# Retention and wave-MLP in one kernel: all batches by chunk pairs, loads in 512-byte rows, transposes moved from TensorE to DMA

## Chip, cores, metric

One core of one Trainium2 chip. The metric is the device time of one launch in microseconds; lower is better.

## The reference, cut to what matters

```python
# retention, for B=4, H=8, S=768, D=64: one state (D x D) per batch and head
state = gamma * state + k_t^T v_t
y_t = (1/sqrt(D)) * q_t @ state
# y becomes x (4, 768, 512); then the wave-MLP block
theta = x @ w_theta
zr, zi = x * cos(theta), x * sin(theta)
u = x + w_tok_r @ zr + w_tok_i @ zi        # over the 768 tokens of a batch
out = u + relu(u @ w_ch)
```

The recurrence is computed in chunks of 128 tokens: A = masked K Q^T inside a chunk, Y = A V, I = the part from the state, S = the update of the state. The MLP block works on 24 tiles of 128 tokens; a tile needs z of all six chunks of its batch.

## The kernel before

Batch 0 is already done by *pairs* of chunks: 256 tokens are loaded as 128 partitions with two neighbouring tokens each, so a DMA row is 512 bytes, and the products use quarters (64 by 64) of the array. Batches 1 to 3 load one chunk at a time in 256-byte rows. One queue (SP) issues nearly all DMA.

```python
def load_chunk(n):                                   # batches 1 to 3
    for name, src in (("kf", k), ("qf", q), ("vf", v)):
        t = io.tile([P, H, D], FT, name=name, bufs=7)
        nc.sync.dma_start(out=t, in_=src[b, :, c * P:(c + 1) * P, :].rearrange("h s d -> s h d"))
def load_pair(g): ...                                # batch 0: "h (p two) d -> p h (two d)"

def att_T(n):                                        # k and q by TensorE: 8 transposes + a copy
    for i, src in enumerate((s["kb"], s["qb"])):
        for j in range(NP):
            nc.tensor.transpose(kq_ps[:, i * NP + j, :], src[:, j * P:(j + 1) * P], ident)
    nc.vector.tensor_copy(kqT, kq_ps)
def att_T_dma(n):                                    # ... by DMA: only n >= 19 (batch 3)
    nc.sync.dma_start_transpose(out=kqT, in_=s["kqb"]...)
# ... x: TensorE for n < 19, DMA after. u: TensorE for tiles m < 12, DMA after.

for s_ in range(last_slot):                          # one chunk and about one tile per slot
    load_chunk(n + 5)                                # loads run five chunks ahead
    moe_U_dma / att_T(n) / att_Z(n - 3) / moe_M(first half) / att_prep(n + 1)
    att_Yinter(n - 1) / att_A(n) / att_Y(n - 1) / moe_M(second half) / moe_O / att_X(n - 2)
```

## Time and profile before

| | before |
|---|---|
| time, median (lowest to highest) | 181.78 us (181.23 to 185.89, 4 runs) |
| profiled span, mean granted clock | 180.0 us, 0.99 |
| PE busy, DVE busy, ACT busy | 91%, 60%, 43% |
| 128x128 transposes on TensorE (k and q, x, u) | 152, 76, 52 |

Engines are named as in the profile: PE is TensorE, DVE VectorE, ACT ScalarE, POOL GpSimd, SP the engine that issues DMA. A step from one PE instruction's start to the next is what it costs; the "busy" length of one is longer (0.38 us for products that start 0.22 us apart). The lines that the argument starts from stand in the prediction.

### The profile page before, as it was taken

To read this page: it belongs to the slowest core of one execution; us is meant where nothing else is said; L and a number is where in the kernel's file an instruction comes from. 1 tells how busy PE (TensorE), PEld (TensorE's weight loads), DVE (VectorE), ACT (ScalarE), POOL (GpSimd) and SP (SyncE) were. 2 spreads that over 40 slices of the span, in tenths; PEclk is the share of its full clock that TensorE was granted. 3 is DMA by queue.
4 is the path that set the end of the run, shared out by engine and by line. 5 is a ranking of instruction groups with operands and counts; after the bars stand their busy time and mean duration, and the time that the engine had idled before them with its cause. 6 is when DMAs were issued, how large, how long until landed. Compare 5 with 4: busy or idle time off the path is not lost.

```text
span 180.0 us, 3837 instructions
## 1 busy us (share of the span) xinstructions
PE 163.8 (91%) x1511; PEld 93.6 (52%) x1538; DVE 107.8 (60%) x153; ACT 77.3 (43%) x143; POOL 74.6 (41%) x102
## 2 busy tenths in 40 slices
PE   7889886796989699999999999999999999999990
PEld 2355563544556365665565556455544544444560
DVE  2266776654754777878676676575645644434441
ACT  6426664451059745746362464346445332200010
POOL 6284557298786687657663562250000000000000
PEclk9999999999999999999999999999999999999997
DMA  4999999999989999999999799945464363334643
GB/s 136 310 329 329 298 364 230 285 303 212 285 181 273 206 218 227 274 256 229 220 244 247 147 228 192 196 87 120 117 117 109 95 103 92 99 94 112 110 127 118
DMA packets 85906, 35.64 MB, mean 198 GB/s; under 512 B 70912, under 2 KB 80384, under 8 KB 85888
## 3 DMA queue, kind: packets, MB, share of 16 engines
q1 hardware_dynamic: 85744, 35.27, 83.7%
q8 instruction: 12, 0.20, 0.5%
q10 hardware_dynamic: 144, 0.13, 0.2%
q14 instruction: 6, 0.05, 0.1%
HBM read 25.69 MB, written 6.29 MB: 178 GB/s over the span
## 4 chain that ended last, share of the span: by engine, by line
PE 82%; DVE 6%; ACT 5%; issue 3%; DVEq 0%; ACTq 0%
PE y_ps L425 31%; PE o_ps L453 11%; PE th_ps L396 11%; PE yT_ps L360 3%; PE at_ps L331 3%; PE y_ps L545 3%; PE kq_ps L202 3%; PE st_ps L368 3%; PE x_ps L393 2%; PE yT_ps L349 2%; PE kq_ps L236 2%; PE u_ps L436 2%; PE y_ps L495 1%; ACT stbd L319 1%; DVE at L255 1%
## 5 line engine op out<-in xcount | busy, mean ns | idle before, releaser
L425 PE MATMUL y_ps<-z,wti 128*128 128x512 bf16 x136 | 51.5, 379 | 0.7 <-issue 0.2
L425 PE MATMUL y_ps<-z,wtr 128*128 128x512 bf16 x127 | 48.1, 379 | 2.5 <-DVE z L407 2.1
L401 ACT ACTIVATE cs<-th_ps,halfpi 128x512 bf16<-128x512 f32 x24 | 16.5, 687 | 35.1 <-PE th_ps L396 32.8
L407 DVE TENSOR_TENSOR z<-cs,x_sb 128x1024 bf16<-128x1024 bf16 x24 | 19.1, 798 | 15.8 <-ACT cs L402 15.8
L335 DVE TENSOR_TENSOR at<-at_ps,mask 128x1024 bf16<-128x1024 f32 x18 | 22.0, 1220 | 6.0 <-PE at_ps L331 6.0
L396 PE MATMUL th_ps<-wth,xT 128*128 128x512 bf16 x90 | 24.0, 379 | 0.3
L453 PE MATMUL o_ps<-wch,uT 128*128 128x512 bf16 x88 | 23.1, 379 | 0.2
L430 DVE TENSOR_TENSOR u<-y_ps,x_sb 128x512 bf16<-128x512 f32 x23 | 15.8, 690 | 12.5 <-PE y_ps L425 12.5
L193 POOL TENSOR_TENSOR vb<-vf,vsc 128x512 bf16<-128x512 f32 x18 | 19.5, 1085 | 6.2 <-PE yT_ps L360 3.5
L456 DVE SCALAR_TENSOR_TENSOR ot<-o_ps,u 128x512 f32<-128x512 f32 x23 | 15.9, 691 | 10.1 <-PE o_ps L453 9.9
L425 PEld LDWEIGHTS <-wti 128*128 128x128 bf16 x138 | 13.5, 98 | 16.2 <-issue 3.6
L191 POOL TENSOR_TENSOR kqb<-qf,qsc 128x512 bf16<-128x512 f32 x18 | 19.7, 1096 | 5.1 <-DMA qf<-in_q_dram 5.0
L425 PEld LDWEIGHTS <-wtr 128*128 128x128 bf16 x138 | 13.5, 98 | 13.5
L319 ACT CAST stbd<-st_ps 64x256 bf16<-64x256 f32 x40 | 14.6, 366 | 11.9 <-PE st_ps L308 11.4
L190 POOL CAST kqb<-kf 128x512 bf16<-128x512 f32 x18 | 11.7, 650 | 15.3 <-PE st_ps L368 9.8
L402 ACT ACTIVATE cs<-th_ps,zerob 128x512 bf16<-128x512 f32 x24 | 16.3, 681 | 0.0
L376 ACT CAST xT<-yT_ps 128x512 bf16<-128x512 f32 x18 | 10.5, 585 | 8.7 <-PE yT_ps L360 7.4
L453 PEld LDWEIGHTS <-uT 128*128 128x128 bf16 x92 | 8.8, 98 | 9.9 <-ACT uT L438 0.2
L468 POOL CAST wrow<-wtok 128x768 bf16<-128x768 f32 x12 | 10.2, 862 | 8.6 <-PE w_ps L475 6.2
L205 DVE COPY kqT<-kq_ps 128x1024 bf16<-128x1024 bf16 x13 | 9.0, 689 | 6.2 <-PE kq_ps L202 6.2
L396 PEld LDWEIGHTS <-xT 128*128 128x128 bf16 x96 | 8.6, 98 | 6.8
L545 PE MATMUL y_ps<-warm 128*128 128x512 bf16 x26 | 9.7, 497 | 1.5 <-DVE warm L124 1.3
(79 smaller groups left out, 195.2 us busy)
## 6 DMA issues: line engine op xcount, KB each, us to landing
out_dram<-ot SPq DMA_DIRECT2D x23, 256.0 KB, 2.3
kf<-in_k_dram SPq DMA_DIRECT2D x18, 256.0 KB, 4.9
qf<-in_q_dram SPq DMA_DIRECT2D x18, 256.0 KB, 5.3
vf<-in_v_dram SPq DMA_DIRECT2D x18, 256.0 KB, 5.5
wtok<-in_moe_w_tok_r_dram SPq DMA_DIRECT2D x6, 384.0 KB, 5.8
wtok<-in_moe_w_tok_i_dram SPq DMA_DIRECT2D x6, 384.0 KB, 5.5
pair<-in_k_dram SPq DMA_DIRECT2D x3, 512.0 KB, 8.1
pair<-in_q_dram SPq DMA_DIRECT2D x3, 512.0 KB, 9.1
```

The lines of the kernel that those rows point to most:

```text
L191: nc.gpsimd.tensor_mul(qb.rearrange(r3, h=H), raw[n, "qf"], _bcast_last(qsc[:, c], D))
L193: nc.gpsimd.tensor_mul(vb.rearrange(r3, h=H), raw[n, "vf"], _bcast_last(vsc[:, c], D))
L319: nc.scalar.copy(stbd[(c + 1) % 2][sl, :, sl], st_ps[b][sl, :, sl])
L335: nc.vector.tensor_mul(at.rearrange("p a j t -> p (a j) t"), at_ps.rearrange("p a j t -> p (a j) t"), _bcast_mid(mask, H))
L396: nc.tensor.matmul(th_ps, s["xT"][:, j, :], wth[:, j, :], start=(j == 0), stop=(j == NP - 1))
L401: nc.scalar.activation(cs[:, 0, :], th_ps, AF.Sin, bias=halfpi, scale=1.0)
L402: nc.scalar.activation(cs[:, 1, :], th_ps, AF.Sin, bias=zerob, scale=1.0)
L407: nc.vector.tensor_mul(zs[b][:, c], st[n]["cs"], _bcast_mid(xs[b][:, c, :], 2))
L425: nc.tensor.matmul(y_ps, wT[r][:, s0, t0 * P:(t0 + 1) * P], zs[b][:, s0, r, :], start=(s0 == 0 and r == 0), stop=(s0 == nT - 1 and r == 1))
L430: nc.vector.tensor_add(u, y_ps, xs[b][:, t0, :])
L453: nc.tensor.matmul(o_ps, mo[m]["uT"][:, j, :], wch[:, j, :], start=(j == 0), stop=(j == nD - 1))
L456: nc.vector.scalar_tensor_tensor(ot, o_ps, 0.0, mo[m]["u"], ALU.max, ALU.add)
```

## The change

The intent: give all batches the pair form that batch 0 has, with one slot per pair (two chunks, two tiles), and take transposes off TensorE, which is busy to the end.

```diff
-    def load_chunk(n): ...            # 256-byte rows, bufs=7 per input
+    def load(n, name):                # any pair, 512-byte rows, 7 buffers in all
+        t = io.tile([P, H, 2 * D], FT, name="pair", bufs=7)
+        nc.sync.dma_start(out=t, in_=src[b, :, 2 * g * P:2 * (g + 1) * P, :].rearrange(
+            "h (p two) d -> p h (two d)", two=2))
+    def flip_dma(n, name):            # k or q of a pair, 128x1024
+        nc.sync.dma_start_transpose(out=t.rearrange("p w j t -> p (w j) t"), in_=...)
+    def x_dma(n):                     # x of a pair, 128x1024
+        nc.sync.dma_start_transpose(out=xs[b][:, 2 * g:2 * g + 2, :]..., in_=st[n, "xT"]...)
-    moe_U (TensorE, m < 12), att_X (TensorE, n < 19), att_T (TensorE, n < 19)
+    # u: moe_U_dma but for the last tile.  x: TensorE only for pairs 0-2.  k, q: TensorE only for pairs 0-3.
-            nc.tensor.matmul(st_ps[b][:, j, :], s["kb"][:, j * P:(j + 1) * P], ...)   # 128x128
+            nc.tensor.matmul(st_ps[b][par * D:(par + 1) * D, j, :], ...)              # 64x64 x4
@@ the slot of pair n (cut to the order in which SP meets its work) @@
+        load(n + 2, "k")
+        for t in done: moe_U_dma(t)          # tiles of the slot before
+        prep(n + 1, "q", PP); prep(n + 1, "v", PP)
+        ret_I(n - 1, 1)
+        ret_A(n, 0); ret_mask(n, 0)          # needs kT, qT of pair n
+        ret_Y(n - 1, 1); ret_S(n - 1, 1); ret_out(n - 1, 0, ...); ret_out(n - 1, 1, ...)
+        x_dma(n - 1)                         # waits for ScalarE's copies of xT
+        load(n + 2, "q")
+        prep(n + 1, "k", K); flip_dma(n + 1, "k")
+        moe_M(mine[0] ...); theta(n - 1, 0); moe_u(mine[0])
+        load(n + 2, "v")
+        flip_dma(n + 1, "q")
+        theta(n - 1, 1); ret_S(n, 0); ret_A(n, 1); ret_mask(n, 1); ret_Y(n, 0); ret_I(n, 0)
+        moe_M(mine[1], 0, nT)
+        zmul(n - 1, 0); zmul(n - 1, 1); moe_u(mine[1])
+        for t in done: moe_O(t); moe_out(t)
```

Slots run from 3 to 12, slots 5 and 6 with one tile. Loads of pairs 5 to 11 are issued in slots 3 to 9. In the prologue the cast of k of pair 2 on ScalarE also moved to an earlier place.

## The prediction

> **What bounds the kernel now.** I read, in this order, the page's table of busy slices, the busy time by windows, the waits, the timeline of TensorE and the list of DMA issues.
>
> ```profile
> PE   7889886796989699999999999999999999999990
> PEclk9999999999999999999999999999999999999997
> DMA  4999999999989999999999799945464363334643
> ```
>
> Each digit is a slice of 4.5 us. From slice 13 (about 58 us) to the end TensorE is never under 90% busy and its clock is full; before that it has holes. The DMA engines are full from 5 us to about 115 us, then half empty. So two resources are full together for the first two thirds, and a change that moves work from one to the other has to be costed on both.
>
> ```profile
> 20.00:40.00 20.00, 15.96 (x238) 10.55 (x240) 14.60 (x20) 11.15 (x19) 11.57 (x12) 1.00 1.12 294
> 60.00:80.00 20.00, 19.60 (x203) 12.16 (x207) 16.04 (x24) 10.71 (x21) 14.39 (x15) 1.00 1.10 240
> 80.00:100.00 20.00, 19.84 (x202) 12.06 (x205) 14.72 (x21) 10.73 (x21) 10.98 (x12) 1.00 1.07 234
> 140.00:160.00 20.00, 19.89 (x118) 9.51 (x119) 9.44 (x14) 5.59 (x10) 0.00 (x0) 1.00 0.41 93
> ```
>
> Columns: stretch, busy time of PE, PEld, DVE, ACT, POOL, then clock, DMA share, GB/s. The full DMA moves 294 GB/s while 512-byte rows (batch 0) are loaded, 234 to 240 with 256-byte rows. In the waits, PE waits 0.2 us in all between 62 and 176 us, and about 9 us between 8 and 62 us, on DVE and ACT results. It does not wait for a load, since loads run up to five chunks ahead. So the end is set by TensorE's work, with DMA hidden by prefetch.
>
> Busy PE is not PE at its peak, so I cost PE from distances between starts:
>
> ```profile
> 21.19 0.42 PE L251 MATMUL at_ps<-kqT 64*64 64x128 bf16 x16 [0.24 <-DVE at L255]
> 21.41 0.42 PE L271 MATMUL yT_ps<-at,kqb 64*64 64x128 bf16 x16
> 21.77 0.40 PE L285 MATMUL yT_ps<-kqT,stbd 128*128 128x128 bf16 x4
> ...
> 103.09 0.61 PE L202 MATMUL kq_ps<-ident,kqb 128*128 128x128 bf16 x8
> 103.54 0.38 PE L425 MATMUL y_ps<-z,wtr 128*128 128x512 bf16 x1
> 103.75 0.38 PE L425 MATMUL y_ps<-z,wti 128*128 128x512 bf16 x1
> ```
>
> Eight transposes hold PE 0.45 us (56 ns each); a 512-column product 215 ns; sixteen products on 64 by 64 tiles 0.22 us, or 0.36 us when the next group has another tile size.
>
> **What the Trainium skill says.** "TensorE: Matmul & The Clock Gate", Part 1: a warm matmul starts every N / 2.4 GHz + 2.5 ns, 215.7 ns for 512 and 55.6 for 128 columns; the trace agrees. "TensorEngine Tiling (Array Packing)", Key Properties: tiles run independently, but a change of tiling mode drains the array; the trace agrees (14 ns per 64 by 64 product, and 0.13 us more at a change). "DMA: Bandwidth & Descriptors", Specifications: line rate wants at least 512 bytes. The trace agrees in direction only: 256-byte rows still reach about 80% of the rate of 512-byte rows. Same page, Queues, rings and completion order: each DMA engine takes descriptors in ring order, so with everything issued from one queue a load issued first delays a transpose issued after it. The kernel before shows it as late landings (below).
>
> **The change on TensorE.** Removed are transposes. Of k and q: 104 + 48 on the page, after it 4 pairs x 16 = 64, so 88 fewer. Of x: 76, then 24 (pairs 0 to 2), 52 fewer. Of u: 52, then 4, 48 fewer. 188 x 56 ns = 10.5 us, all on the path. The attention work is about equal: for two chunks before, A 2 x 0.33, Y 2 x 0.35, S 2 x 0.23, I 0.45 = 2.3 us; for a pair after, 6 groups of 16 at 0.22, three changes of mode and I 0.45 = 2.2 to 2.5. Products y, theta and o do not change. A steady slot (one pair, two tiles) is then 24 x 0.216 + 8 x 0.216 + 8 x 0.216 + 2.3 = 10.9 us, and I add 0.3 for theta waiting behind the ACT copies of xT: 11.2, where the kernel before takes 11.8 to 12.6 for two chunks. DVE sheds 11 kq copies of 0.69 and 13 x copies of 0.41 (about 13 us), ACT trades 12 uT copies (7.0 us) for k casts of 1.04 per pair; neither was the bound. With nothing else, 181.7 - 10.5 = about 171 us.
>
> **The change on DMA.** Costs over 16 engines from the packet records of the trace before. Saturated between 60 and 70 us, 8230 packets of 256 bytes: 16 x 10 us / 8230 = 19.4 ns apiece, so a chunk load (1024 packets) is 1.24 us. Between 4 and 24 us, taking out 512 packets of 2 KB at 85 ns and 320 of 3 KB at 121 ns, 8318 packets of 512 bytes cost 28.6 ns, so a pair load (1024 packets) is 1.83 us. Half the packets, three quarters of the time: loads of batches 1 to 3 fall from 54 x 1.24 = 67 us to 27 x 1.83 = 49 us.
>
> A transpose of 128x512 is 512 packets of 256 bytes at about 20 ns, 0.64 us; 128x1024 is 1.28. Before: 5 + 16 / 2 = 13 of the large size, 17 us. After: 16 flips, 9 of x and 23 u, 25 x 1.28 + 23 x 0.64 = 47 us. So the DMA gains 18 us in loads and pays 30 us in transposes: its total grows by about 12 us, and it was already full until 115 us.
>
> ```profile
> kf<-in_k_dram SPq DMA_DIRECT2D x18, 256.0 KB, 4.9
> pair<-in_k_dram SPq DMA_DIRECT2D x3, 512.0 KB, 8.1
> uT<-u SPq DMA_TRANSPOSE x11, 2.4
> kqT<-kqb SPq DMA_TRANSPOSE x5, 3.3
> ```
>
> The last column is issue to landing: 1.2 us of work takes 4.9 us to land behind a full queue, and the transposes, which before ran mostly after the queue had emptied, land in 2.4 to 3.3. After the change the flips of pairs 4 to 10 sit between the loads of two pairs further on.
>
> A steady slot asks the DMA for three loads 5.5, two flips 2.56, x 1.28, two u 1.28, two outputs of 0.70 (128 packets of 87 ns): 12.0 us, against 11.2 on PE. In slots 5 and 6, which hold one tile each, PE needs only 9.0 and 7.5 us. So from slot 4 to slot 9 the first product of each slot, A, should wait for kqT.
>
> The DMA's chain up to the flip of pair 10, after which no load is left: first work by about 3 us; loads of pairs 0 to 4 27.5; the two 1 MB weights 5.6 and eight token rows 7.8; loads of pairs 5 to 11 38.4; four token rows 3.9; fourteen flips 17.9; six x 7.7; ten u 6.4; eight outputs 5.6. The sum is 124 us. Then PE: slots 10 and 11 at 11.2, slot 12 at 9.2, five tail tiles at 3.45, and 9.7 us for the last tile as in the trace before: 58.6. Span 182.5, and time is 1.7 over span (181.7 for 180.0): **184**. If packets of 512 bytes cost 25 ns, as the very first ones do, once transposes that do not touch HBM are mixed in, 21 loads save 0.23 us each, so 179.5.
>
> **Rivals.** (1) PE stays the bound and the gain arrives whole: about 171, or 168 if the reordered first 60 us lose some of their 9 us of waits. For it: the removed work is certainly on the path, and the prologue shows the DMA full without PE waiting for a load. Against: those loads had five chunks of lead, while a flip has one slot, and its DMA needs a load queue to drain first. (2) DMA is the bound from slot 4 to 9, as computed: 179 to 184. For it: DMA share 1.07 to 1.12 already. Against: saturated costs of 512-byte packets are from a stage that mixed weights in. (3) DMA is the bound and the single queue also idles, as SP waits in order (outputs wait for DVE at the slot's end before the next k load; the x transpose waits for ACT), about 1 us in each of six slots; with PE holes long enough to lower its clock: 186 to 190. Against it: in DMA-bound slots the backlog covers these waits.
>
> **Range and chances.** I weigh rival 2 most, at its lower end for unsure packet costs, and give rival 1 a third: the point is 180.5, range 173 to 187. Faster by over 2% means under 178.0: 0.33. Within 2%: 0.48. Slower means over 185.3: 0.19.
>
> **What would show it.** Right: about 188 fewer 128x128 transposes; PE waits of 1 to 5 us of A on kqT's DMA in slots 4 to 6; DMA share near 1 until about 120 us, with 300 GB/s or less; flips landing in 4 us or more; slots of 11.5 to 12.5 us while loads last, near 11 after. Wrong: DMA share falling well under 1 before 90 us, flips landing in under 4 us with no PE wait on them, and slots of 11 us from the start; then the time is near 171. If slots are long though no wait on a DMA is seen, the attention groups on 64 by 64 tiles or the ACT copies cost more than I took.

## The result

The change takes **203.86 us** (202.17 to 203.94, 4 runs) against 181.78: 1.121 times as long, 95% interval 1.114 to 1.128. Ratios here and below are the mean time of one kernel's fast runs over that of the other's of the same rounds, so not quite the ratio of the medians. It lies outside the predicted range of 173 to 187. The outputs are right.

The page's slices of the change (5.0 us each), which answer to the first lines of the prediction:

```profile
PE   7698479867599894198696896994999999799991
PEclk9999957996999999859699699997899999999999
DMA  5999999999998989989699899999445244434443
```

TensorE now has holes until slice 28 (about 140 us) and its clock falls in many of them, while the DMA is full exactly that long. Two windows (columns as before) show a stretch with loads and one without:

```profile
80.00:100.00 20.00, 12.69 (x159) 6.47 (x163) 7.95 (x9) 7.51 (x14) 8.17 (x8) 0.76 0.96 228
140.00:160.00 20.00, 19.36 (x224) 9.82 (x227) 9.76 (x13) 11.23 (x21) 0.00 (x0) 0.96 0.42 94
```

PE's timeline has the wait at the head of each slot. The first product of pair n, A, waits for its transposed k and q:

```profile
84.64 0.64 PE L202 MATMUL at_ps<-kqT 64*64 64x128 bf16 x16 [6.45 <-DMA kqT<-kqb]
96.70 0.42 PE L202 MATMUL at_ps<-kqT 64*64 64x128 bf16 x16 [1.85 <-DMA kqT<-kqb]
110.68 0.50 PE L202 MATMUL at_ps<-kqT 64*64 64x128 bf16 x16 [2.23 <-DMA kqT<-kqb]
```

The list of DMA issues, to set beside that of before: the transposes of k and q land in 5.2 us where they took 3.3, those of u in 2.6.

```profile
pair<-in_k_dram SPq DMA_DIRECT2D x12, 512.0 KB, 5.7
uT<-u SPq DMA_TRANSPOSE x23, 2.6
kqT<-kqb SPq DMA_TRANSPOSE x16, 5.2
x_sb<-xT SPq DMA_TRANSPOSE x9, 3.2
```

And the chain that ended last, for slot 7, in order of time (start, length, what). It is a closed loop: A starts the slot, its results let ScalarE work, SP issues the k transpose and a load behind that, then the q transpose, which lands 5.7 us later and lets the next A start, 14.0 us after the first.

```profile
96.70 0.42 PE at_ps L202 x16
...
102.09 0.69 ACT cs L297
102.78 1.38 SPq L189
...
104.25 0.53 SPq L79
...
104.89 5.66 DMA kqT<-kqb
...
110.68 0.50 PE at_ps L202 x16
```

The link from ScalarE to SP is better read in SP's own timeline. The chain names `cs` at 102.09, but of ScalarE's work the k transpose needs only the cast of k, which ended at 100.80. What holds it back is SP's order: the x transpose starts at 99.93, when ScalarE's copies of xT end (99.91), and a load and the k transpose stand behind it.

```profile
99.93 1.25 SPq L278 DMA_TRANSPOSE x_sb<-xT  x1
101.23 0.58 SPq L79 DMA_DIRECT2D pair<-in_q_dram  x1
101.92 2.23 SPq L189 DMA_TRANSPOSE kqT<-kqb  x1
104.25 0.53 SPq L79 DMA_DIRECT2D pair<-in_v_dram  x1
104.89 2.86 SPq L189 DMA_TRANSPOSE kqT<-kqb  x1
```

**What the DMA engines did.** I counted the packet records between the starts of slots 4 and 10 (here and in all counts below) in bins of 0.1 us. *Work* is the packets at the prediction's costs (19.4 ns for 256 bytes, 28.6 for 512, 85 for 2 KB, 121 for 3 KB, over 16 engines; all others, at 5 ns for 4 bytes and 300 and 600 for fetches of 8 and 16 KB, add under 0.8 us). *Idle* are bins in which the engines hold fewer than 5 packets on average. *Stalled* are bins in which they hold 5 or more but finish less than 40% of what they could. Packets are booked at their end, so the columns need not add up, and another limit than 5 (2 or 8) shifts some 3 us between the last two.

| kernel, window | length | work | idle | stalled |
|---|---|---|---|---|
| before, 20 to 110 us | 90 | 86.6 | 2.5 | 3.5 |
| the change, 54 to 138 us | 84 | 70.7 | 7.2 | 12.0 |

The full digits of the DMA line hide this: an engine that holds a packet counts as busy whether or not the packet moves. The kernel before gets 96% of the packet work out of its full stretch, the change 84%.

### The profile page after: what moved, and what is told of

Its sections match the earlier page's. It is cut to its first block, busy times and chain, and to the rows that moved or that the text cites. A ratio compares the mean times of both kernels' runs of the same rounds, so it can differ in the third digit from the quotient of the medians.

```text
span 200.5 us, 4447 instructions
## 1 busy us (share of the span) xinstructions
PE 162.3 (81%) x1831; PEld 87.0 (43%) x1857; DVE 97.7 (49%) x127; ACT 79.1 (39%) x136; POOL 64.2 (32%) x81
## 4 chain that ended last, share of the span: by engine, by line
PE 37%; DMA 26%; SPq 12%; issue 10%; ACT 6%; POOL 4%; DVE 2%; DVEq 0%; ACTq 0%; POOLq 0%
DMA kqT<-kqb 19%; PE y_ps L315 16%; PE th_ps L293 7%; SPq L79 6%; PE o_ps L333 5%; DMA pair<-in_k_dram 4%; POOL kqb L173 4%; SPq L189 3%; PE at_ps L202 3%; PE st_ps L256 2%; ACT stbd L264 2%; ACT cs L297 2%; PE yT_ps L225 2%; DMA x_sb<-xT 2%; ACT xT L273 1%
## 5 line engine op out<-in xcount | busy, mean ns | idle before, releaser
L315 PE MATMUL y_ps<-z,wtr 128*128 128x512 bf16 x137 | 55.3, 404 | 3.3 <-DVE z L303 2.0
L315 PE MATMUL y_ps<-z,wti 128*128 128x512 bf16 x121 | 48.3, 399 | 0.3 <-issue 0.3
L209 DVE TENSOR_TENSOR at<-at_ps,maskp 128x1024 bf16<-128x1024 f32 x24 | 29.3, 1222 | 24.3 <-PE at_ps L202 24.3
L173 POOL TENSOR_TENSOR kqb<-pair,qscp 128x512 bf16<-128x512 f32 x20 | 21.6, 1097 | 51.8 <-DMA pair<-in_q_dram 43.8
L173 POOL TENSOR_TENSOR kqb<-pair,vscp 128x512 bf16<-128x512 f32 x24 | 26.4, 1120 | 10.9 <-DMA pair<-in_v_dram 9.5
L293 PE MATMUL th_ps<-wth,xT 128*128 128x512 bf16 x93 | 26.5, 407 | 1.4 <-ACT xT L273 0.7
L202 PE MATMUL at_ps<-kqT 64*64 64x128 bf16 x384 | 11.4, 232 | 19.2 <-DMA kqT<-kqb 17.5
L273 ACT CAST xT<-yT_ps 128x512 bf16<-128x512 f32 x23 | 15.3, 732 | 20.0 <-PE yT_ps L225 19.8
L202 PEld LDWEIGHTS <-kqT 64*64 64x64 bf16 x384 | 8.1, 112 | 22.4 <-issue 18.6
L167 ACT CAST kqb<-pair 128x1024 bf16<-128x1024 f32 x12 | 12.6, 1050 | 3.9 <-DMA pair<-in_k_dram 3.8
```

Of the source, the lines that this page charges most:

```text
L173: engines[two].tensor_mul(dst[:, two], src[:, two], _bcast_last(sc[:, 2 * g + two], D))
L202: nc.tensor.matmul(at_ps[half, par, j, :], kT[rows, two, j, half], qT[rows, :, j, half], start=(j == 0), stop=(j == NP - 1), skip_group_ch ...
L209: nc.vector.tensor_mul(at.rearrange("p a j t -> p (a j) t"), at_ps.rearrange("p a j t -> p (a j) t"), _bcast_mid(maskp[:, two].rearrange(" ...
L273: copy(st[n, "xT"][:, a].rearrange("e j (i w) -> e j w i", w=2), st[n, "y"][a].rearrange("e j (w i) -> e j w i", w=2))
L293: nc.tensor.matmul(th_ps, st[n, "xT"][:, a, j, :], wth[:, j, :], start=(j == 0), stop=(j == NP - 1))
L315: nc.tensor.matmul(y_ps, wT[r][:, s0, t0 * P:(t0 + 1) * P], zs[b][:, s0, r, :], start=(s0 == 0 and r == 0), stop=(s0 == nT - 1 and r == 1))
```

## The experiments

Fifteen kernels, all derived from the change. "Before" ran in the same rounds each time (medians 183.1 to 184.8 us there). Starts of A, in us, mark the slots:

| kernel | median us | ratio to before (95%) | slot 4 | 5 | 6 | 7 | 8 | 9 | 10 |
|---|---|---|---|---|---|---|---|---|---|
| the change | 203.86 | 1.121 (1.114 to 1.128) | 54.0 | 68.0 | 84.6 | 96.7 | 110.7 | 124.9 | 138.4 |
| order | 203.92 | 1.116 (1.105 to 1.127) | 49.6 | 64.4 | 76.9 | 90.9 | 104.1 | 120.6 | 134.2 |
| z_only | 203.91 | 1.109 (1.098 to 1.121) | 54.5 | 69.7 | 86.7 | 99.0 | 112.9 | 127.4 | 140.9 |
| order_z | 192.24 | 1.052 (1.037 to 1.067) | 49.9 | 64.4 | 77.2 | 87.8 | 102.4 | 115.5 | 126.2 |
| flips_pe_k2 | 183.23 | 1.002 (0.993 to 1.010) | 46.4 | 61.2 | 72.7 | 82.5 | 93.9 | 107.3 | 119.7 |
| best_u | 179.59 | 0.986 (0.979 to 0.993) | 47.5 | 62.3 | 73.8 | 82.5 | 93.9 | 106.2 | 117.6 |

### order: the k and q transposes first in SP's queue

```diff
+        prep(n + 1, "k", K); flip_dma(n + 1, "k")     # ahead of every load of the slot
+        prep(n + 1, "q", PP); flip_dma(n + 1, "q")
         load(n + 2, "k")
 ...
-        flip_dma(n + 1, "k") / flip_dma(n + 1, "q")   # at their old places
```

> Edit: in each slot the k and q transposes of the next pair are issued ahead of the x transpose and of all loads; the DMA's work is the same. Theory Q (one queue: each slot is a closed loop from A through the copies of xT, the x transpose, a load, the k transpose, a load, the q transpose to the next A): the wait of A on kqT goes nearly away, slots 4 to 9 shrink from 14 us to about 12, the clock recovers, time 186 to 191 us. Theory W (the DMA's work and its stalls fill the slot, in any order): slots stay near 14 us and time stays within 3 us of 203.9.

203.92 us: nothing gained. But the reason is not the one that theory W gives. PE's wait on kqT did go, and another took its place. From the waits of this run (engine, line, for whom: us, times, longest):

```profile
DVE z L303 <- DMA x_sb<-xT: 41.4, 9, 7.3
...
PE y_ps L315 <- DVE u L322: 12.9, 7, 4.2
...
PE at_ps L202 <- DMA kqT<-kqb: 2.6, 3, 1.3
```

Its chain in slot 8 shows the link: x lands late, VectorE, which works in order, stands at z until then, so u comes late, and PE cannot start the next y in the bank that u reads.

```profile
115.74 6.24 DMA x_sb<-xT
...
122.68 0.68 DVE z L303
123.36 0.61 DVE u L322
...
124.02 0.38 PE y_ps L315
```

In the change, z waits for x only 4.8 us in all. In both orders the transpose that is put last holds PE. At this point I read that as "the DMA is too slow in any order", which order_z later refuted. The edit has a side effect that I overlooked: ScalarE's cast of k now stands ahead of its copies of xT, and with it the wait for k's load (32.0 us in all; 3.8 in the change).

### act_loads: loads on another queue

```diff
-        load(n + 2, "k"); ... load(n + 2, "q"); ... load(n + 2, "v")
+        load(n + 2, "k", nc.scalar); ...              # issued by ScalarE
```

> Edit: the loads of pairs 5 to 11 are issued from ScalarE's queue, the transposes stay on SP. Theory Q: transposes no longer stand behind a load in the same ring; kqT lands in about 3.5 us instead of 5.2, and each slot loses 2 to 3 us; time 187 to 193 us. Theory W: the same bytes, so 201 to 206 us. A third outcome, ScalarE blocked while it issues into a full ring, would show as longer waits of theta and xT on ACT.

203.43 us (1.111, interval 1.098 to 1.124). PE waits 20.0 us on kqT, which now lands in 6.0 us. So the place behind a load in one ring (the queue of one issuing engine) is not by itself the cause: on another ring, the loads still use the same engines at the same time.

### flips_pe and xu_pe: transposes back to TensorE

```diff
 flips_pe:  -flip_dma(n + 1, "k"), flip_dma(n + 1, "q")
            +flip(n + 1, "k"), flip(n + 1, "q")        # around moe_M(mine[1])
 xu_pe:     -x_dma(n - 1), moe_U_dma(t)                # in the slots
            +x_pe(n - 1, a), moe_U(t)
```

> Edit: k and q of pairs 4 to 11 are transposed by TensorE (16 transposes and two copies of 0.69 us on DVE per pair), x and u stay on DMA. Theory Q: no DMA on the path to A, slots of about 12.1 us (11.2 + 0.9 on PE), time 182 to 188. Theory W: the DMA's work per slot falls from 12 to 9.4 us, the same time; this run sizes what the k and q transposes cost together, not which of the two it is.

> Edit: x and u are transposed by TensorE in the slots as in the kernel before, k and q stay on DMA. Theory Q: the wait of SP on xT is gone and SP issues 4 us less per slot, so the q transpose is issued earlier: slots near 12 us, A's wait mostly gone, time 186 to 192. Theory W: 2.6 us less DMA work per slot, slots 11.5 to 12.5, time 186 to 192. If DMA work were not the matter and only the order of flips behind loads (not the wait on xT), the slots would stay at 13 or more and the time above 196.

flips_pe takes 186.97 us (1.025, interval 1.011 to 1.038), 17 us less than the change; xu_pe 200.45 (1.099, 1.092 to 1.106), only 3 less, though both take about 2.6 us of DMA work out of a slot. In xu_pe the DMA is idle for 14.9 of the 80 us between slots 4 and 10, yet the slots stay at 12 to 15 us: the k and q transposes still hold slots 4, 6 and 7 (by 2.9, 1.6 and 2.9 us), and later PE, with 16 more transposes in its slot, waits on ScalarE's copies of xT and uT. So equal DMA work does not mean equal time. What counts is whether it lies on the loop from A to A.

### plain_copy and no_loads: is it the transposing?

```diff
 plain_copy (wrong result on purpose):
-        nc.sync.dma_start_transpose(out=t..., in_=st[n, name]...)
+        for w in range(2):                            # the same 256 KB in the same 256-byte runs
+            nc.sync.dma_start(out=t.rearrange("p w j t -> p (w j) t")[:, w::2, :],
+                              in_=st[n, name][:, w].rearrange("p (j t) -> p j t", j=NP))
+        # and q is scaled by 1e-14, so that theta stays small with the wrong products
 no_loads (wrong result on purpose):
-        load(n + 2, ...)
+        raw[n + 2, ...] = raw[4, ...]
```

> Wrong result on purpose. Edit: the k and q transposes of pairs 4 to 11 become plain copies of the same 256 KB from SBUF to SBUF, written in runs of 256 bytes (so again 1024 packets each), issued at the same places; q is scaled down so that theta stays in range. The trace of the change shows 70.8 us of packet work (at the packet costs of the prediction) taking 84 us between 54 and 138 us, with many stretches of 0.3 to 1.8 us in which hardly a packet ends. Theory X (a transpose in flight among loads stalls the DMA engines): with plain copies the stalls go, slots 4 to 9 shrink from 14 us to 11.5 to 12.5, time 188 to 193. Theory W (the packet work alone, whatever it is): slots stay at 13.5 to 14.5, time 200 to 206.

> Wrong result on purpose. Edit: pairs 5 to 11 load nothing and use the data of pair 4; all transposes stay. Theory X as I form it (stalls come of transposes that meet loads): no stalls of over 0.3 us but those at an instruction fetch, slots at PE's 11 us, time 174 to 181. If transposes stall the engines by themselves, with no load in flight, stalls stay and time is over 183. Theory W predicts 174 to 181 too (6.5 us of DMA work per slot); the two are told apart by the plain copies.

plain_copy takes 200.89 us (1.099, 1.089 to 1.109): the forecast of theory X fails. PE waits 18.8 us on kqT, the DMA stalls for 10.3 us of 85 (12.0 of 84 in the change) and idles 5.2. For the time, a copy of k and q that transposes nothing costs nearly the same. For the stalls the run decides less, since x and u are still transposed by DMA in it: eleven of the twelve stalls of 0.3 us or more begin while such a transpose is between issue and landing. In the 38.9 us with one in flight the DMA stalls for 7.5 us; in the 39.5 us with copies of k or q in flight and no transpose, for 1.8.

no_loads takes 177.43 us (0.970 of before, 0.963 to 0.978; its fast runs give the ratio). So the change without its later loads is faster than the kernel before, by about half of the 10.5 us forecast for TensorE. Its DMA still stalls for 8.6 us of 66. Six stalls are of 0.3 us or more (0.6 to 1.4 us), and each begins within 0.8 us after the start of a fetch of instructions (a packet of 8 or 16 KB on the DMA engines). In the change only four of fifteen have such a fetch within 0.9 us before them. A fetch alone does not stall the engines: none of the eleven fetches among the loads of before, from 20 to 110 us, is followed within 0.9 us by a stall of over 0.3 us.

### flips_pe_k2: the prologue

```diff
-    prep(2, "k", K)          # ScalarE: stands until k of pair 2 has landed (22 us)
     keep_busy(2)
     ret_S(1, 0)              # its copies of the state come behind that on ScalarE
 ...
     ret_I(1, 0)
+    prep(2, "k", K)
     ret_S(1, 1)
```

> Edit on flips_pe: in the prologue the cast of k of pair 2 on ScalarE is moved behind the copies of the state of chunk 2, so that PE does not wait 2.2 us for them and its clock does not fall (0.77 granted between 20 and 35 us). If that wait and the clock are what flips_pe loses in its first 50 us (its slot 4 starts at 50.6 us), the time falls by 3 to 5 us, to 182 to 184; if loads set the prologue's pace, by under 1 us.

183.23 us (1.002, 0.993 to 1.010), 3.7 us under flips_pe. The first line is the wait in the change's timeline; the windows from 20 to 35 us of flips_pe and flips_pe_k2 show the clock (third number from the end) with and without it.

```profile
23.85 0.44 PE L256 MATMUL st_ps<-kqb 64*64 64x64 bf16 x16 [2.24 <-ACT stbd L264]
```

```profile
20.00:35.00 15.00, 11.56 (x209) 8.19 (x206) 9.47 (x13) 8.22 (x15) 7.13 (x7) 0.77 1.11 324
```

```profile
20.00:35.00 15.00, 11.88 (x245) 8.02 (x238) 12.13 (x16) 11.04 (x19) 8.59 (x9) 1.00 1.10 322
```

### late_dma: the last two pairs by DMA again

```diff
+            if n >= 9: flip_dma(n + 1, "k"); flip_dma(n + 1, "q")    # pairs 10 and 11
```

> Edit on flips_pe_k2: the k and q transposes of pairs 10 and 11, issued when at most one pair's loads are left, go back to DMA: 32 transposes off PE, 1.8 us. Theory X: they meet few loads, so the gain comes whole, 180 to 182.5. If any use of DMA transposes for k and q costs more than it saves, 183 or more.

183.60 us (1.010, 0.998 to 1.021): a miss of the forecast, and not told apart from flips_pe_k2 (1.002). Pair 10's transposes are issued in slot 9, beside the loads of pair 11, and A waits 2.9 us for them at the head of slot 10, more than the 1.8 us saved.

### order_z and z_only: slack for x as well

```diff
-        zmul(n - 1, 0); zmul(n - 1, 1)            # before moe_u(mine[1])
 ...  in the next slot, behind ret_mask:
+        zmul(n - 2, 0); zmul(n - 2, 1)            # z one slot later; cs gets a fourth buffer
```

order_z has this on top of order; z_only has it alone.

> Edit on order: the product z of a pair is put one slot later on VectorE (behind the first mask of the next slot), so that a late x transpose no longer holds back u and with it PE. In order the k and q transposes came in time and x came late, with the slots as long as before. Theory L (latency: each order puts one landing on the path of an engine that works in order, and slack for all three would remove it): slots of 12 to 12.5 us, time 188 to 193. Theory W2 (the DMA's work of a slot, 12 us, plus about 2 us of stalls and idle time, is the pace whatever waits for it): slots 13.5 to 14.5 on average, time 198 to 204, with the wait moved again, to kqT or to a load.

> Edit on the change: only the later z of order_z. Theory L (both slacks are needed, since k and q still stand behind x and two loads in each slot): slots stay near 14 us, time 200 to 205. If the later z alone gives the 11.7 us, the order of the transposes never mattered: 190 to 194.

order_z takes **192.24 us** (1.052, 1.037 to 1.067): 11.7 us less than order, with the same transfers. z_only takes 203.91, as the change does, with 22.6 us of waits on kqT. So neither edit does anything alone, and together they give half of the loss back. In order_z PE waits 1.2 us on kqT and z 5.2 us on x. Between slots 4 and 10 the DMA does 68.8 us of work in 76 us; idle time is down from 7.2 to 1.2 us, stalls are 12.9. Its DMA line has no gap any more while loads last:

```profile
DMA  5999999998999999999999999999966052534443
```

Theory L holds for the first part of the loss, and theory W2 is refuted. What remains has a wait of its own, which I first overlooked. PE's largest wait is now for xT, which ScalarE copies only after it has waited for the load of k (the side effect of order):

```profile
ACT kqb L167 <- DMA pair<-in_k_dram: 31.7, 9, 5.2
...
PE th_ps L293 <- ACT xT L273: 9.8, 7, 2.9
```

### order_z_k2: the prologue again

> Edit on order_z: the prologue's k cast of pair 2 behind the state copies, as in flips_pe_k2 (where it gave 3.7 us). If PE sets the pace of the first 50 us, the time falls by 2.5 to 4 us to 188 to 190. If the DMA's chain does (it is full from 5 us on, and slots 4 to 9 follow it), by under 1 us: 191.5 to 193.

191.75 us (1.048, 1.039 to 1.057): no gain, where the same edit (that of flips_pe_k2) gave flips_pe 3.7 us. Its clock is full between 20 and 35 us, but A of slot 4 then waits 2.3 us for kqT, and slot 10 starts at 127.3 us, not earlier than in order_z. So the time gained in the prologue turns into waits later (PE waits 12.4 us for xT here, 9.8 in order_z). That agrees with a pace set outside PE from the prologue on, but the run does not show by what.

### warm: the clock

```diff
+        fill = {4: 8, 6: 24, 7: 7, 8: 8, 9: 8, 10: 7}.get(n, 0)
+        for _ in range(fill): nc.tensor.matmul(w_ps, warm[:, 0:P], warm, ...)    # before ret_A(n, 0)
```

> Edit on the change: products of zeros fill most of the time in which PE waits at the start of slots 4 and 6 to 10 (7 to 24 of 0.22 us), so its clock need not fall. If the fallen clock (0.93 on average) lengthens the path, the time falls by 3 to 6 us, to 198 to 201; if the DMA sets the pace of the slots and the slow products lie in its shadow, by 0 to 2 us.

201.34 us (1.104, 1.092 to 1.117), 2.5 us under the change, between the two forecasts and at the edge of what the runs resolve. The mean clock of the profiled runs rose only from 0.93 to 0.96. The slowed clock is a small part.

### all_pe: no SBUF-to-SBUF transfer in the slots

```diff
 flips_pe and xu_pe together, with the prologue of flips_pe_k2
```

> Edit: no SBUF-to-SBUF transfer in the slots: k, q, x and u all on TensorE, loads in 512-byte rows as in the change, prologue as in flips_pe_k2. If the stalls come with SBUF-to-SBUF transfers, the stretches of over 0.3 us without a packet ending go from about 12 us to under 3 us between 46 and 130 us. PE gains 16 + 8 + 8 transposes per slot against the change (1.8 us), slots 12.7 to 13.2, time 184 to 189. If loads of 512-byte rows stall by themselves, 6 us or more of stalls remain.

The stalls go: 2.7 us of 80, beside 12.0 of 84 in the change. The loads are the same, so the stalls come with the transposes by DMA, the only transfers from SBUF to SBUF in the change. flips_pe_k2 shows the same within one run: 9.4 us of stall in the 45.4 us with an x or u transpose in flight, 0.6 in the 27.9 us without. It is not only that the engines have less to do: no_loads, with 20.8 us of idle DMA in 66, still stalls for 8.6. The time was a miss: 194.09 us (1.059, 1.053 to 1.066), worse than predicted, as slots take 13 to 17 us (10 with one tile in slot 6); between its transposes PE waits for VectorE's and ScalarE's copies out of PSUM. The DMA has room to spare:

```profile
DMA  5999999999993391493906809630020020533443
```

### best_z and best_u: a version that keeps what pays

```diff
 flips_pe_k2
+ z one slot later (as in order_z)                                        # best_z
+ for t in done: moe_U_dma(t)   ahead of   load(n + 2, "k")               # best_u
+ k, q of pair 11 by DMA, in slot 10, where no load is in flight          # best_u
```

> Edit on flips_pe_k2: the later z of order_z. In flips_pe_k2 PE still waits 1.5 and 0.8 us for u, which waits for z, which waits for x. Gone with the edit: 180.5 to 182.5, about 1.5 us under flips_pe_k2. If DMA stalls move the wait to uT, no gain: 183.

> Edit on best_z: the u transposes are issued ahead of the slot's first load (two waits of O on uT, 3 us with the first slots), and k and q of pair 11, for which no load is in flight, are transposed by DMA (0.9 us of PE). 178.5 to 181, below the kernel before by 1 to 2%. If the transposes cost as much in waits as they save on PE, 181 to 183.

best_z takes 180.95 us (0.990, 0.974 to 1.005), best_u **179.59 us** (0.986, 0.979 to 0.993): 1.4% under the kernel before and 12% under the change. By a 2% measure that counts as the same as before; the interval lies below 1. Its page and its waits of PE on DMA:

```profile
PE   7889788898899898998999999999999999699991
...
DMA  4999999999999999989998696898963261444343
```

```profile
PE o_ps L333 <- DMA uT<-u: 1.4, 1, 1.4
```

## Why the prediction was wrong, point by point

- **The work taken off TensorE: right.** The change's profile counts 64 transposes of k and q, 24 of x and 4 of u, 188 fewer, as forecast. Slot 11, with no load left, took 11 us. no_loads, with no load in the way, keeps about half of the gain: 177.4 us.
- **The bound from slot 4 to 9: right in kind.** PE waits for kqT at the head of the slots, by up to 6.5 us, with the DMA full until 140 us. Rival 1 was wrong.
- **The work of the DMA: right in size.** A slot's packets came to 10.6 to 11.4 us of work in slots 6 to 8 (12.0 forecast for two tiles, less for the one-tile slots and their outputs).
- **The step that failed is the sum of the DMA's chain: "The sum is 124 us".** It ran the packets without a pause up to the flip of pair 10; slot 10 started at 138.4 us. It took the saturated cost per packet from stages that had only loads. The change's 70.7 us of work took 84, in which the engines stalled for 12.0 us and idled for 7.2.
- **The sentence that let it pass: "in DMA-bound slots the backlog covers these waits".** It does not. SP reaches the x transpose only once ScalarE has copied xT, behind it stand the k transpose, a load and the q transpose, and the last takes 5.7 us to land. So a slot is a loop of 14 us with idle DMA in it. Giving k, q and x slack together (order_z) takes 11.7 us off. Rival 3 named the loop but gave it 1 us per slot and an upper end of 190; in slot 7 of the change, 14.0 us long, I count 1.6 us of idle time and 1.9 us of stall. The sum also left out SP's own time: a transpose takes SP 1.2 us to issue even with an empty queue (u in the last third of before) and up to 3.0 among loads (132.67 us in the change).
- **The stalls were in no rival.** They come with transposes by DMA (all_pe, and the stretches with and without one in flips_pe_k2). The trace of before had them too, in its last third (1.2 to 1.4 us each at 115.1, 145.3 and 169.5 us), where PE waited for none of them; I did not look for them.
- **The rest.** The reordered prologue costs flips_pe 3.7 us; rival 1 had assumed that the reordering could only help. Undone in order_z it gained nothing (order_z_k2); in the change itself that was not run. The fallen clock costs about 2.5 us (warm). From slot 10 on the change takes 62.1 us (200.5 less 138.4) where 58.6 was forecast: slot 10, with transposes still in flight, took 12.4 us for 11.2; the rest of this I did not trace.

**What stays open.** Why transposes by DMA stall the engines is not settled. In no_loads every long stall begins at an instruction fetch; in the change most do not, and those lie where loads and transposes mix. No run took the stalls away while keeping both. As to order_z's remaining 8 to 9 us over flips_pe_k2, it is shown that they hang on how k and q are transposed: order_z_k2 and best_z have the same prologue and the same later z and differ only in that and in the order that goes with it, and they take 191.75 and 180.95 us. What in it costs the time is not shown. Three candidates stand beside each other in order_z, and no run separates them: the stalls (12.9 us of 76), ScalarE's wait for the loads of k ahead of xT (9.8 us of waits of PE), and SP, which is issuing DMA for 70.2 of the 76 us (66.0 of 84 in the change). act_loads took the loads off SP, but only in the change's order.

## What to carry to other kernels

A resource that is full in the profile but waited for by nobody, because its work is prefetched far ahead, has no room for work with a short deadline: cost the deadline (issue, queue, landing) as a loop through every in-order engine it touches, beside the sum of the work. When a reordering gains nothing, look at which wait took the place of the old one before concluding that the resource is too slow (work moved ahead on an in-order engine takes its own wait along); here two edits, each worth nothing alone, gave 11.7 us together. And a busy digit of a DMA engine does not say that packets move: count the packets that end.

## What the Trainium skill lacked or had wrong

- "DMA: Bandwidth & Descriptors", Latency and other measured facts, gives 261 GB/s for DMA transposes, from one kernel, and about 350 to 400 for a contiguous case. Here a 128x512 transpose in the last part of the change (u, issued at 180.76 us) moved its 131 KB in 512 packets within 0.78 us, with the end of one output beside it: 168 GB/s. What decided this case has no figure there for this chip and these sizes: SP took 1.23 us to issue that transpose and 1.26 for one of 128x1024 (x at 154.45 us), and up to 3.0 among loads; landing took 3.1 us (x at 154.45 us), and 5.2 among loads.
- No page has the stalls within one core: in windows of 66 to 86 us, in the runs with transposes by DMA in every slot, the engines stalled for 9 to 15 us, against 2.7 us in 80 without them (all_pe).
- "TensorE: Matmul & The Clock Gate", Why this matters for your kernels, advises against gaps of over about 3 us. Here products that were 0.22 us apart at 91 us were 0.43 us apart after a wait of 1.85 us (the one at 96.70 us), so a shorter gap was enough; after a wait of 2.22 us (54.03 us) they stayed 0.22 apart:

```profile
98.53 0.63 PE L315 MATMUL y_ps<-z,wtr 128*128 128x512 bf16 x1
98.96 0.63 PE L315 MATMUL y_ps<-z,wti 128*128 128x512 bf16 x1
```
